# Regions on 512-byte starts, a constant made on GpSimd, first weights from the fifth unit on, and passes over 3, 5 and 8 slices, in an attention and two-layer MLP kernel

## The chip, the cores and the metric

One core of one Trainium2 chip runs the kernel. The metric is device time in microseconds (us), the median of the runs. [...]

## What is computed

```python
# 4 batches, 8 heads, 576 positions, head size 64
scores = (q @ k.T) / sqrt(64)
out = (scores * D) @ v            # D[i,j] = gamma_h**(i-j) for i >= j, else 0
x = out as [2304 tokens, 512]
h = x @ moe_w_in                  # 512 -> 2048
y = (h * sigmoid(1.702 * h)) @ moe_w_out     # 2048 -> 512
h2 = y @ moe2_w_in                # 512 -> 1024
s = h2 * softmax(h2)
z = (s - mean(s)) / sqrt(var(s) + 1e-6) * g_ln
return z @ moe2_w_out             # 1024 -> 512
```

All arrays are float32. The weights come to the device as float64 in 32-bit halves.

## The kernel before

**Attention.** There are 16 units, one for two heads of one batch. A unit is cut into four chunks of 128 positions and a rest of 64. `st0` scales v on ACT (L286, L287). `st2` makes the scores of the chunks on PE (L334) and masks them on DVE (L338). `states` makes the chunk states on PE (L298), which ACT scales out of PSUM (L304), and `st1` runs the scan over chunks on DVE (L314). `st4` puts the output together on PE (L355 with the masked scores, L367 to L378 with the scanned states), and DVE writes it into `xb` (L385, L390). In the loop over u in `run`, PE runs st2(u), L355 of unit u-1, states(u), and then L367 of unit u-1, which needs the scan of u-1, hence L304 of u-1. ACT, which takes its instructions in order, has st0(u+1) between the two: L304(u-1) stands behind it. Five input buffers (`NU`) hold units; unit u+4 is loaded when unit u-1 is done.

**First MLP layer.** The 2048 hidden columns are 16 weight slices. A slice's raw halves arrive in `wraw`. Three DVE instructions make float32 of 512 raw columns (`convert`: L208, L211, L214; six pieces for a slice), ACT rounds the 128x1024 result to float32r (L231, the "high" part w) and GpSimd subtracts for the "low" part (L236, twice 512 columns). This ACT and GpSimd work is called the split of a slice here. The pieces stand in a list `bg`; `background(n)` takes n DVE pieces from its front, and with them any splits that follow. Weights 0 to 7 are converted from the start; weights 8 to 15 replace them later. The tokens are six blocks of 384. A pass (`GENS`) takes all six blocks over a range of slices; a step is one slice of one block: 12 matmuls for h (L425), ACT sigmoid (L429), DVE product, high and low part (L430, L434, L435, into `gs`), then, one step later, 12 matmuls for y (L452). At a block's end y leaves PSUM (ACT L458 in the first pass, DVE L460 after it). The next block's x is split on ACT and GpSimd (L406, L407) in the last two steps of a block.

**Second layer.** h2 (L528) uses seven products in place of eight, with `ys` tiles as stationary operand (162 + 108 + 54 + 54 matmuls of 512 columns). After the normalization come transposes (L589), and the output o (L616) with the transposed tile `zs` as stationary operand: 17 token tiles with 24 matmuls of 512 columns, and the last with 48 of 256.

**Order and placement.** The order is written out by hand; the SP queue issues every load in program order. `mem` is one tile that is cut into regions by the table `_M` (constants, y, g, the attention buffers "att", three slots "t").

Of the kernel before, what the change touches and what calls it, by code (L numbers as in the profile page):

```python
# [9 lines left out]
F32 = mybir.dt.float32  # L10
# [7 lines left out]
B, H, S, D = 4, 8, 576, 64  # L18
NP = H // 2
# [4 lines left out]
P = 128  # L24
# [6 lines left out]
FH = NF // 2  # L31
GENS = ((0, 4), (4, 8), (8, 16))
NTT = NT // P
# [12 lines left out]
for _name, _w in (  # L46
    ("half", 1), ("g_ln", FB), ("vdec", NP * 3), ("step", NP), ("tri2", LAST), ("tri", CH), ("qdec", NP * CH),
    ("scan", NP * D * NCH),
):
    _CC[_name] = (_n, _n + _w)  # L50
    _n += _w

CCONST, _n_consts = _CC["scan"][0], _n


def constants():
# [22 lines left out]

    put("scan", step[:, :, None, None] * np.ones((D, 1)) * (np.arange(NCH) > 0))  # L80
    put("vdec", vdec / math.sqrt(D))
# [10 lines left out]

SLICE = 2 * DM
_M = {}
_n = 0
for _name, _w in (
    ("c", CCONST), ("y", NB * KB * TB), ("g", 2 * TB),
    ("att", 2 * CATT + 2 * NCH * D + 4 * NCH * CH + 2 * LAST), ("t", 3 * SLICE),
):
    _M[_name] = _n  # L100
    _n += _w
# [38 lines left out]
class Build:  # L140
    def __init__(self, tc, ctx, att, consts, ident_in, w1, w2in, w2out, out):
# [5 lines left out]
        self.wp = pool("wp")  # L147
        self.ctx, self.early, self.early_s = ctx, ExitStack(), ExitStack()
        self.gs = self.early_s.enter_context(
            tc.tile_pool(name="gsp", bufs=1, side="right", reuse_waits="tile")  # L150
# [26 lines left out]
    def load_decays(self, p, n):  # L177

        for name, at, w in (("scan", SCAN_AT, D * NCH), ("qdec", _M["c"] + _CC["qdec"][0], CH)):
            lo = _CC[name][0] + p * w  # L180
            self.load(at + p * w, self.const_in[:, lo:lo + n * w])

# [126 lines left out]
    def st1(self, u):  # L309

        st = self.un(u)[1]
        g = self.at(SCAN_AT + u % NP * D * NCH, D * NCH)
        st = self.at(ST_AT + (u % 2) * NCH * D, NCH * D)
        self.nc.vector.tensor_tensor_scan(st, g, st, 0.0, ALU.mult, ALU.add)  # L314
# [100 lines left out]
    def emit_h(self, gen, j, f, lo_engine, hi_act=False):  # L415
# [5 lines left out]
        for k in range(KB):  # L421
            x = self.xst[gen, j, k]
            w = slice(k * P, (k + 1) * P)
            for a, b in ((hi, 0), (lo, 0), (hi, 1)):
                nc.tensor.matmul(h[:, 0:TB], a[:, w], x[:, b], start=(n == 0), stop=(n == 3 * KB - 1))  # L425
                n += 1
        g = self.at(_M["g"] + (f % 2) * TB, TB)
        gs = self.gs[:, f % 2 * 2:f % 2 * 2 + 2]
        nc.scalar.activation(g, h[:, 0:TB], AF.Sigmoid, scale=1.702)  # L429
# [7 lines left out]
    def emit_y(self, gen, j, f):  # L437
        nc = self.nc
        hi, lo = self.w[f]
        gs = self.gs[:, f % 2 * 2:f % 2 * 2 + 2]  # L440
        first, last = f == GENS[gen][0], f == GENS[gen][1] - 1
# [183 lines left out]
    def run(self):  # L625
# [20 lines left out]
        for part in range(3):  # L646
            self.load_unit(0, part)
            if part == 0:
                self.load_consts()
        self.load_decays(0, 1)  # L650
        self.load_unit(1, 3)
        self.load_unit(1, 2)
        self.load_decays(1, NP - 1)
        for u in range(2, NU):
            self.load_unit(u, 3)
            self.load_unit(u, 2)
            if u != 3:
                load_w()

# [16 lines left out]
        for u in range(1, last + 2):  # L676
            if u <= last:
                self.st2(u)
                if u > 1:
                    self.background(1)  # L680
            else:

                while 0 not in self.split:
                    self.background(1)
                self.emit_h(0, 0, 0, nc.vector, True)
# [9 lines left out]
            if u < last - 1:  # L695
                self.st0(u + 2)
            if u % 2 == 0 or u > NU + 2:
                self.background(1)
# [5 lines left out]

        steps = [(g, j, f) for g, lo_hi in enumerate(GENS) for j in range(NB) for f in range(*lo_hi)]
        prev, held = None, []
        for g, j, f in steps:
            fl, n = f - GENS[g][0], GENS[g][1] - GENS[g][0]
# [6 lines left out]
            if g == 1 and j == 0 and fl == 1:  # L715

                for i in range(4):
                    first, *rest = self.split_weight(FH + i, T_LATER[i])
# [198 lines left out]
```

## Time and profile before

| | |
|---|---|
| median of 3 runs | 698.78 us (698.7 to 698.8) |
| the profiled execution's own time | 697.44 us |
| its span, first to last instruction | 695.7 us |
| busy: PE, DVE, ACT, POOL | 676.7, 512.0, 235.9, 225.8 us |
| DMA moved | 49.92 MB |

The profiled execution is 1.34 us under the median. PE is matmuls, PEld its weight loads, which run beside them; L numbers are lines of the kernel before. Up to about 75 us the core works on attention, to 482 us on the first layer, from there on the second.

### The profile page before, as it was taken

What the parts mean: (1) busy time and instruction counts of PE and PEld (TensorE: products, weight loads), DVE (VectorE), ACT (ScalarE), POOL (GpSimd) and SP (SyncE); (2) the same over time, 40 slices, a digit from 0 to 9 for tenths busy, and PEclk for the clock granted to TensorE, in tenths of its full rate; (3) what the DMA queues carried; (4) which work ended last, traced back from release to release, by engine and by line L of the source; (5) the groups of instructions that cost most, each with busy time, mean ns of one, the idle gap of its engine ahead of it and who ended that gap; (6) DMA issues with size and microseconds to landing.
All of it is one profiled execution on the core that took longest, in us unless ns stands there. A gap on an engine that the chain in (4) does not pass through costs nothing.

```text
span 695.7 us, 11260 instructions
## 1 busy us (share of the span) xinstructions
PE 676.7 (97%) x4454; PEld 629.6 (91%) x4454; DVE 512.0 (74%) x868; ACT 235.9 (34%) x496; POOL 225.8 (32%) x235
## 2 busy tenths in 40 slices
PE   7899999999999999999999999999998999999998
PEld 7888899999999999999999999998776788888887
DVE  2899847768788876636777777788698877877780
ACT  3554243333322233221212121254444424452331
POOL 0222154442232386520202030488633314331300
PEclk9999999999999999999999999999999999999999
DMA  9999500003232210001232210000000000000001
GB/s 325 419 341 373 201 1 1 1 1 103 81 91 91 78 44 1 1 1 60 62 96 64 84 61 1 1 1 4 2 15 16 16 30 32 30 16 16 30 32 46
DMA packets 13733, 49.92 MB, mean 72 GB/s; under 512 B 1520, under 2 KB 2544, under 8 KB 12272
## 3 DMA queue, kind: packets, MB, share of 16 engines
q1 hardware_dynamic: 13680, 49.20, 19.9%
q8 instruction: 35, 0.57, 0.3%
q14 instruction: 18, 0.15, 0.1%
HBM read 44.48 MB, written 4.72 MB: 71 GB/s over the span
## 4 chain that ended last, share of the span: by engine, by line
PE 80%; DVE 11%; ACT 3%; DMA 2%; issue 2%; POOL 1%; SPq 0%; POOLq 0%; DVEq 0%; ACTq 0%
PE yp L452 28%; PE h L425 27%; PE o L616 13%; PE h L528 9%; DMA mem<-in_att 2%; PE zT L589 2%; DVE mem L338 2%; DVE mem L568 1%; POOL xs L407 1%; DVE mem L314 1%; DVE mem L573 1%; DVE mem L208 1%; DVE mem L214 1%; DVE wraw L211 1%; ACT mem L566 1%
## 5 line engine op out<-in xcount | busy, mean ns | idle before, releaser
L452 PE MATMUL yp<-gs,w 128*128 128x384 f32 x1152 | 216.9, 337 | 0.7 <-DVE gs L435 0.6
L425 PE MATMUL h<-xs,w 128*128 128x384 f32 x1152 | 216.9, 337 | 0.6 <-POOL xs L407 0.3
L452 PEld LDWEIGHTS yp<-gs,w 128*128 128x128 f32 x1152 | 200.4, 188 | 3.4 <-DVE mem L460 1.8
L425 PEld LDWEIGHTS h<-xs,w 128*128 128x128 f32 x1152 | 201.0, 188 | 2.2 <-POOL xs L407 2.1
L407 POOL TENSOR_TENSOR xs<-xb,xs 128x384 fp32r<-128x384 f32 (+1 forms) x96 | 87.3, 934 | 253.2 <-ACT xs L406 253.2
L429 ACT ACTIVATE mem<-h 128x384 f32<-128x384 f32 x96 | 47.3, 493 | 267.8 <-PE h L425 267.6
L430 DVE TENSOR_TENSOR mem<-h,mem 128x384 f32<-128x384 f32 x96 | 53.4, 556 | 87.5 <-ACT mem L429 87.2
L616 PE MATMUL o<-w,zs 128*128 128x512 f32 (+1 forms) x456 | 105.1, 386 | 0.6 <-ACT zs L598 0.4
L616 PEld LDWEIGHTS o<-w,zs 128*128 128x128 f32 x456 | 81.1, 188 | 18.4 <-ACT zs L598 0.8
L435 DVE TENSOR_TENSOR gs<-mem,gs 128x384 fp32r<-128x384 f32 x96 | 80.3, 837 | 11.1 <-ACT gs L432 2.3
L236 POOL TENSOR_TENSOR w<-mem,w 128x512 fp32r<-128x512 f32 x40 | 55.9, 1422 | 64.9 <-ACT w L231 54.2
L434 DVE CAST gs<-mem 128x384 fp32r<-128x384 f32 x92 | 53.1, 577 | 9.1 <-PE yp L452 0.5
L489 POOL TENSOR_TENSOR ys_s<-mem,ys_s 128x256 fp32r<-128x256 f32 x36 | 33.9, 952 | 58.2 <-ACT ys_s L488 58.2
L528 PE MATMUL h<-wt,ys_s 128*128 128x512 f32 x162 | 41.6, 392 | 0.7 <-DVE mem L534 0.7
L534 DVE TENSOR_TENSOR mem<-h,mem 128x512 f32<-128x512 f32 x36 | 24.6, 688 | 22.6 <-PE h L528 13.4
L528 PEld LDWEIGHTS h<-wt,ys_s 128*128 128x128 f32 x162 | 30.2, 188 | 7.6 <-DVE mem L534 1.1
L406 ACT CAST xs<-xb 128x384 fp32r<-128x384 f32 (+1 forms) x96 | 35.5, 431 | 0.0
L576 POOL TENSOR_TENSOR mem<-mem 128x1 f32<-128x1 f32 x18 | 10.1, 559 | 69.3 <-DVE mem L575 61.5
L599 DVE TENSOR_TENSOR zs<-zT,zs 128x512 fp32r<-128x512 f32 x36 | 23.1, 683 | 8.8 <-ACT zs L598 8.8
L568 DVE TENSOR_TENSOR mem<-mem 128x1024 f32<-128x1024 f32 x18 | 25.3, 1406 | 4.9 <-ACT mem L566 4.9
L528 PE MATMUL h<-wb,ys_a 128*128 128x512 f32 x108 | 27.5, 390 | 0.0
L231 ACT CAST w<-mem 128x1024 fp32r<-128x1024 f32 x20 | 20.8, 1049 | 19.1 <-DVE mem L214 13.7
(78 smaller groups left out, 723.4 us busy)
## 6 DMA issues: line engine op xcount, KB each, us to landing
mem<-in_att SPq DMA_DIRECT2D x11, 1120.0 KB, 8.4
wraw<-in_w SPq DMA_DIRECT2D x16, 512.0 KB, 9.5
mem<-in_w SPq DMA_DIRECT2D x16, 512.0 KB, 3.7
out<-mem SPq DMA_DIRECT2D x17, 256.0 KB, 2.0
mem<-in_w2in SPq DMA_DIRECT2D x8, 512.0 KB, 3.8
mem<-in_w2out SPq DMA_DIRECT2D x8, 512.0 KB, 3.7
mem<-in_att SPq DMA_DIRECT2D x5, 544.0 KB, 8.0
mem<-in_att SPq DMA_DIRECT2D x4, 576.0 KB, 9.3
```

What stands on the lines that cost most here:

```text
L236: nc.gpsimd.tensor_tensor(lo[:, c], w[:, c], f32(hi[:, c]), ALU.subtract)
L406: nc.scalar.copy(t[:, 0, done:done + n], x)
L407: nc.gpsimd.tensor_tensor(t[:, 1, done:done + n], x, f32(t[:, 0, done:done + n]), ALU.subtract)
L425: nc.tensor.matmul(h[:, 0:TB], a[:, w], x[:, b], start=(n == 0), stop=(n == 3 * KB - 1))
L429: nc.scalar.activation(g, h[:, 0:TB], AF.Sigmoid, scale=1.702)
L430: nc.vector.tensor_tensor(g, h[:, 0:TB], g, ALU.mult)
L434: nc.vector.tensor_copy(gs[:, 0], g)
L435: lo_engine.tensor_tensor(gs[:, 1], g, f32(gs[:, 0]), ALU.subtract)
L452: nc.tensor.matmul(o, a[:, w], gs[:, b], start=(first and i == 0), stop=(last and i == 2))
L489: nc.gpsimd.tensor_tensor(ys[:, 1], src, f32(ys[:, 0]), ALU.subtract)
L528: nc.tensor.matmul(o, a[:, l, k], m[:, w], start=(start and i == 0), stop=(stop and i == 5), skip_group_check=True,)
L616: nc.tensor.matmul(o[:, 0:n], z[:, a, k], b[:, c:c + n], start=(k == 0 and i == 0), stop=(k == FB - 1 and i == 2),)
```

## The change

1. **Regions.** `mem` begins at byte 16512 of a partition. Each region of `_M` now begins at a multiple of 512 bytes (before: 128 bytes past one for the constants, 484 bytes past one for y, g, att and t). A pad of 480 bytes at the right end moves the tiles allocated there: `gs`, the x splits `xs`, `zs` and the last weight w19 (before: 480 bytes past a multiple of 512; now 0). The tiles of `w`, `wraw`, `xb` and `ys` lay at multiples of 512 bytes before and do so now.
2. **scan constants.** The 512 KB factor table of the scan is no longer loaded (before: 128 KB ahead of unit 1 and 384 KB ahead of unit 2). GpSimd fills it with one memset of 128x1024 and four copies of 128x64x3.
3. **First weights.** The first two loads of weight halves come after units 2 to 4, not between them. Background pieces begin at u = 4, one for an odd u and two for an even one (before: u = 2, two for u = 2, 4, 6 and each u from 8, else one).
4. **Passes** over slices 0 to 2, 3 to 7 and 8 to 15 (before 0 to 3, 4 to 7, 8 to 15), with g and gs buffers by the parity of the step, not of the slice.

```diff
-GENS = ((0, 4), (4, 8), (8, 16))
+GENS = ((0, 3), (3, 8), (8, 16))
+STEPS = [(g, j, f) for g, lo_hi in enumerate(GENS) for j in range(NB) for f in range(*lo_hi)]
+BUF = {s: i % 2 for i, s in enumerate(STEPS)}
...
-    ("scan", NP * D * NCH),
...
+LINE = 128
+MEM_SHIFT = 96
+RIGHT_PAD = 120
...
+    _n += (MEM_SHIFT - _n) % LINE
     _M[_name] = _n
...
+        pad = ctx.enter_context(tc.tile_pool(name="pad", bufs=1, side="right"))
+        self.pad = pad.tile([P, RIGHT_PAD], F32, name="pad")
...
-        for name, at, w in (("scan", SCAN_AT, D * NCH), ("qdec", _M["c"] + _CC["qdec"][0], CH)):
-            lo = _CC[name][0] + p * w
-            self.load(at + p * w, self.const_in[:, lo:lo + n * w])
+        lo = _CC["qdec"][0] + p * CH
+        self.load(_M["c"] + lo, self.const_in[:, lo:lo + n * CH])
+
+    def fill_scan(self):
+
+        nc = self.nc
+        nc.gpsimd.memset(self.at(SCAN_AT, NP * D * NCH), 0.0)
+        for p in range(NP):
+            g = self.at(SCAN_AT + p * D * NCH, D * NCH).rearrange("r (e c) -> r e c", c=NCH)
+            step = self.const("step")[:, p:p + 1].unsqueeze(2).to_broadcast([P, D, NCH - 1])
+            nc.gpsimd.tensor_copy(g[:, :, 1:], step)
...
-        g = self.at(_M["g"] + (f % 2) * TB, TB)
-        gs = self.gs[:, f % 2 * 2:f % 2 * 2 + 2]
+        b = BUF[gen, j, f]
+        g = self.at(_M["g"] + b * TB, TB)
+        gs = self.gs[:, b * 2:b * 2 + 2]
...
+        self.fill_scan()
         self.load_decays(0, 1)
...
             self.load_unit(u, 2)
-            if u != 3:
-                load_w()
+        load_w()
+        load_w()
...
-                if u > 1:
+                if u > 3:
                     self.background(1)
...
-            if u % 2 == 0 or u > NU + 2:
+            if u > 3 and u % 2 == 0:
                 self.background(1)
...
-                for i in range(4):
+                for i in range(GENS[0][1]):
                     first, *rest = self.split_weight(FH + i, T_LATER[i])
```

The SP queue at the start of the program, before (`in_att` are units: two rows for one unit; `in_consts` constants; `in_w` a half slice; the kernel's own lines):

```order
L171 DMA mem<-in_consts 128x256
L171 DMA mem<-in_consts 128x128
L171 DMA mem<-in_att 128x1152
L171 DMA mem<-in_att 128x1088
L171 DMA mem<-in_consts 128x768
L171 DMA mem<-in_consts 128x384
L171 DMA mem<-in_att 128x1152
L171 DMA mem<-in_att 128x1088
L195 DMA wraw_91<-in_w 128x1024
L171 DMA mem<-in_att 128x1152
```

and of the change, from the same place (the pair of 1152 and 1088 columns is units 1, 2, 3, 4 in turn):

```order
L179 DMA mem<-in_consts 128x128
L179 DMA mem<-in_att 128x1152
L179 DMA mem<-in_att 128x1088
L179 DMA mem<-in_consts 128x384
L179 DMA mem<-in_att 128x1152
L179 DMA mem<-in_att 128x1088
L179 DMA mem<-in_att 128x1152
L179 DMA mem<-in_att 128x1088
L179 DMA mem<-in_att 128x1152
L179 DMA mem<-in_att 128x1088
L211 DMA wraw_95<-in_w 128x1024 x2
```

The rows of 256 and 768 constant columns are gone, and the half slice that stood ahead of unit 3 stands behind unit 4.

DVE in the first pass, the end of one block of tokens and the begin of the next, before (h1_2 and h1_3 are the block's last two steps, h2_0 the next block's first, wraw5 and wraw6 slices in conversion):

```order
L430 TENSOR_TENSOR mem_60<-h1_2_1227,mem_60 128x384
L434 CAST gs_67<-mem_60 128x384
L435 TENSOR_TENSOR gs_67<-mem_60,gs_67 128x384
L211 SCALAR_TENSOR_TENSOR wraw5_96<-wraw5_96,mem_60 128x512
L214 SCALAR_TENSOR_TENSOR mem_60<-wraw5_96 128x512
L430 TENSOR_TENSOR mem_60<-h1_3_1258,mem_60 128x384
L434 CAST gs_67<-mem_60 128x384
L435 TENSOR_TENSOR gs_67<-mem_60,gs_67 128x384
L430 TENSOR_TENSOR mem_60<-h2_0_1293,mem_60 128x384
L434 CAST gs_67<-mem_60 128x384
L435 TENSOR_TENSOR gs_67<-mem_60,gs_67 128x384
L208 TENSOR_SCALAR mem_60<-wraw6_97 128x512
```

and of the change (h1_2 is the last of three steps):

```order
L446 TENSOR_TENSOR mem_60<-h1_2_1195,mem_60 128x384
L450 CAST gs_71<-mem_60 128x384
L451 TENSOR_TENSOR gs_71<-mem_60,gs_71 128x384
L227 SCALAR_TENSOR_TENSOR wraw4_99<-wraw4_99,mem_60 128x512
L230 SCALAR_TENSOR_TENSOR mem_60<-wraw4_99 128x512
L446 TENSOR_TENSOR mem_60<-h2_0_1232,mem_60 128x384
L450 CAST gs_71<-mem_60 128x384
L451 TENSOR_TENSOR gs_71<-mem_60,gs_71 128x384
L224 TENSOR_SCALAR mem_60<-wraw5_100 128x512
L227 SCALAR_TENSOR_TENSOR wraw5_100<-wraw5_100,mem_60 128x512
```

A block still carries the six pieces of one slice, but over three steps: the fourth step, which had no piece behind it, is gone.

## Rows read from the trace of the kernel before

**Rows 1.** Page, part 1: busy us, share of the span, instructions.
```profile
PE 676.7 (97%) x4454; PEld 629.6 (91%) x4454; DVE 512.0 (74%) x868; ACT 235.9 (34%) x496; POOL 225.8 (32%) x235
```
**Rows 2.** The chain that ended last: start us, us, what ran.
```profile
100.43 2.08 PE yp L452 x12
102.51 2.08 PE h L425 x12
...
571.97 5.59 PE o L616 x24
577.56 0.87 PE zT L589 x8
578.43 5.58 PE o L616 x24
584.02 9.57 PE h L528 x42
```
**Rows 3.** Windows: PE, PEld, DVE, ACT, POOL busy, PEclk, DMA share, GB/s.
```profile
5.00:35.00 30.00, 25.58 (x448) 23.10 (x446) 19.32 (x40) 15.45 (x33) 4.73 (x5) 1.00 1.02 404
93.00:110.00 17.00, 16.68 (x96) 16.12 (x95) 11.09 (x18) 7.25 (x18) 7.59 (x9) 1.00 0.00 0
545.00:690.00 145.00, 145.00 (x702) 120.03 (x701) 105.40 (x186) 56.76 (x118) 36.31 (x47) 1.00 0.07 26
```
**Rows 4.** Timeline of PE, attention: start us, us, instruction [idle before it <-releaser].
```profile
9.28 1.16 PE L334 MATMUL s<-mem 64*128 64x128 f32 x16 [0.55 <-DMA mem<-in_att]
13.32 0.99 PE L367 MATMUL o<-mem 64*64 64x128 f32 x12 [0.89 <-DVE mem L314]
14.66 1.16 PE L334 MATMUL s<-mem 64*128 64x128 f32 x16
23.04 0.99 PE L367 MATMUL o<-mem 64*64 64x128 f32 x12 [1.41 <-DVE mem L314]
28.62 1.16 PE L334 MATMUL s<-mem 64*128 64x128 f32 x16
36.14 0.98 PE L367 MATMUL o<-mem 64*64 64x128 f32 x12 [0.94 <-DVE mem L314]
37.47 1.16 PE L334 MATMUL s<-mem 64*128 64x128 f32 x16
41.39 1.16 PE L334 MATMUL s<-mem 64*128 64x128 f32 x16
71.44 1.16 PE L334 MATMUL s<-mem 64*128 64x128 f32 x16
79.05 0.99 PE L367 MATMUL o<-mem 64*64 64x128 f32 x12 [0.28 <-DVE mem L314]
```
**Rows 5.** Timeline of ACT, attention, the same columns.
```profile
19.66 1.06 ACT L286 ACTIVATE mem<-mem 128x256 f32<-128x256 f32 x2 [2.80 <-DMA mem<-in_att]
21.27 0.71 ACT L304 ACTIVATE mem<-T,mem 128x256 f32<-128x256 f32 x1
22.45 1.06 ACT L286 ACTIVATE mem<-mem 128x256 f32<-128x256 f32 x2 [0.47 <-DMA mem<-in_att]
...
33.15 1.05 ACT L231 CAST w<-mem 128x1024 fp32r<-128x1024 f32 x1 [1.66 <-DVE mem L214]
34.10 0.74 ACT L304 ACTIVATE mem<-T,mem 128x256 f32<-128x256 f32 x1
```
**Rows 6.** Waits: who for whom, us in total, times, longest.
```profile
ACT mem L286 <- DMA mem<-in_att: 18.2, 11, 4.7
ACT w L231 <- DVE mem L214: 13.7, 4, 5.7
```
**Rows 7.** DMA issues: how often, KB each, median us to landing.
```profile
wraw<-in_w SPq DMA_DIRECT2D x16, 512.0 KB, 9.5
mem<-in_consts SPq DMA_DIRECT2D x1, 384.0 KB, 7.1
mem<-in_consts SPq DMA_DIRECT2D x1, 128.0 KB, 4.6
```
**Rows 8.** Sources L236 and L435: count, ns min/median/max, first and last start.
```profile
L236 POOL TENSOR_TENSOR w<-mem,w x40: 1269/1307/2270, 34.3 to 497.7; 128x512 fp32r<-128x512 f32 x40
L435 DVE TENSOR_TENSOR gs<-mem,gs x96: 557/561/1568, 81.4 to 479.2; 128x384 fp32r<-128x384 f32 x96
```
**Rows 9.** Timeline of DVE and POOL in one block of the first pass.
```profile
97.55 0.36 DVE L434 CAST gs<-mem 128x384 fp32r<-128x384 f32 x1
...
100.10 2.56 POOL L236 TENSOR_TENSOR w<-mem,w 128x512 fp32r<-128x512 f32 x2 [4.33 <-ACT w L231]
...
101.66 1.22 DVE L434 CAST gs<-mem 128x384 fp32r<-128x384 f32 x1
```

More of the change, by code (lines that the diff above doesn't have):

```diff
@@ L51 @@
     _n += _w
-CCONST, _n_consts = _CC["scan"][0], _n
+CCONST = _n_consts = _n
 def constants():
@@ L78, in constants @@
     put("step", step)
-    put("scan", step[:, :, None, None] * np.ones((D, 1)) * (np.arange(NCH) > 0))
     put("vdec", vdec / math.sqrt(D))
@@ L309, in st1 @@
     def st1(self, u):
-        st = self.un(u)[1]
         g = self.at(SCAN_AT + u % NP * D * NCH, D * NCH)
@@ L439, in emit_y @@
         hi, lo = self.w[f]
-        gs = self.gs[:, f % 2 * 2:f % 2 * 2 + 2]
+        b = BUF[gen, j, f]
+        gs = self.gs[:, b * 2:b * 2 + 2]
         first, last = f == GENS[gen][0], f == GENS[gen][1] - 1
@@ L702, in run @@
             load_w()
-        steps = [(g, j, f) for g, lo_hi in enumerate(GENS) for j in range(NB) for f in range(*lo_hi)]
         prev, held = None, []
-        for g, j, f in steps:
+        for g, j, f in STEPS:
             fl, n = f - GENS[g][0], GENS[g][1] - GENS[g][0]
```

## Prediction

> **What bounds the kernel now.** Read the page's busy times first: PE works 676.7 us [rows 1] of a span of 695.7, so at most some 19 us stand in its gaps, and a change gains only by closing gaps or by making matmuls themselves shorter. The chain of waits then shows where PE runs without a gap: in the first layer twelve matmuls follow each other every 2.08 us, 173.3 ns each, y and h in turn [rows 2], and the window from 545 us on is all PE [rows 3]. Two places are left. One is the attention, where from 5 to 35 us PE is busy 25.58 of 30 us while the DMA engines have no pause (share 1.02, 404 GB/s) [rows 3]. The other, 482 to 545 us, is untouched by the change.
>
> In the attention, look at the starts of L334, one for each unit [rows 4]. The best pitch is 3.92 us (37.47 to 41.39, units 7 and 8). From unit 1 (9.28) to unit 5 (28.62) four pitches took 19.34, so 3.66 too much: 1.46 in the first, 2.20 in the next three. From unit 5 to unit 15 (71.44) ten took 42.82, 3.62 too much. PE waits in L367 for the scan (23.04, 36.14, 79.05 [rows 4]); the scan waits for ACT's L304, and L304 stands behind another ACT instruction. Early that is st0 of the next unit, which waits for its load: ACT was idle 2.80 us until 19.66, and L304 came at 21.27 [rows 5]. Later it is a split: L231 waited 1.66 us for DVE's last piece of the slice, ran 1.05 us, and L304 followed at 34.10 [rows 5]. Both kinds have their line in the waits: 18.2 us for loads, 13.7 us for four splits [rows 6].
>
> **The change, part by part.** The sum is made against the profiled execution, 697.44 us, 1.34 under the median of 698.78.
>
> *Loads.* Gone are 128 KB ahead of unit 1 and 384 KB ahead of unit 2; a half slice of 512 KB moves from ahead of unit 3 to behind unit 4 (sizes: [rows 7]). At 404 GB/s [rows 3] that is 0.32 us earlier for unit 1, 1.3 for unit 2, 2.6 for units 3 and 4, and 1.3 for unit 5, which queues behind the moved half as before. The queue passed is SP's alone; its loads of the halves wait for nothing there. PE's wait at 9.28 was for a load, so unit 1 starts 0.3 earlier. The excess of 1.46 stays: there ACT waits for unit 1's v, which comes only as much earlier as PE itself. The waits of st0 that ended at 19.66 and 22.45 [rows 5] end at about 17.1 and 19.9. L304 then follows 1.6 us later, at 18.7 and 21.5, and its scan some 1.5 us after that, while PE asks for them at about 20.9 and 24.8: L367 stands 1.33 us ahead of the next unit's start (36.14 to 37.47 [rows 4]), so 2.59 after its own at the best pitch, and units 3 and 4 now start at 18.3 and 22.2. So the 2.20 go but for about 0.2 at unit 5. Term: -0.3 - 2.2 + 0.2 = **-2.3 us**. Ends: -4.0 if the first pitch also becomes 3.92; 0 if the waits only change hands.
>
> *Constants on GpSimd.* The nearest row is GpSimd's 512 columns in 1.27 to 2.27 us [rows 8], a subtraction with two inputs. By it the memset of 1024 columns takes 2.5 to 4.5 us and four copies of 192 columns 1.9 to 3.4 together. GpSimd had no work then, the step column comes with the second load of the queue, and the first scan's user waited until 13.32 [rows 4]. Term: **0**, covered by that idle time; if the cover is gone, the first units slip by what it is late, at most a few tenths. No gain of its own remains beside the bytes counted above.
>
> *Pieces and splits.* Up to the end of attention DVE now does 18 pieces, not 25, and ACT three splits, not four: slices 0 to 2 are all that the first block needs. Splits now fall behind the last pieces of slices 0, 1 and 2, in the turns of units 7, 11 and 15. The four splits account for the 3.62 us above and the 0.28 at 79.05 [rows 4], about 1.0 each. One fewer gives 1.0, thinner pieces in the late turns perhaps 0.2 more: **-1.2 us**. Ends: 0, if three splits in a thinner list stall as long as four; -3.9, if none stalls.
>
> *Passes.* The steps and matmuls are the same in number; block ends too. What moves is the conversion of slices 3 to 7 into the first pass. A block there has three steps, 3 x 4.16 = 12.48 us, not 16.64, and still carries six pieces, one split and one x split. In the window of one such block DVE was busy 11.09 us for 18 instructions [rows 3], four steps of three and six pieces; 15 of 18 make 9.2 of 12.48 us. It fits, but the slack shrinks, and where GpSimd runs L236 the cast behind it takes 1.22 us and not 0.36 [rows 9]. y of a step begins a whole step after its h has ended, with another y and h between (the chain's turns [rows 2]), so most of this is hidden. I allow 0.1 us in each of five blocks: **+0.5 us**. Ends: 0 and the rival below. The parity buffers alternate as before, cost 0, hidden by the same alternation; if they didn't, h would wait for y in the odd passes.
>
> *Regions.* Do matmuls care where their operands begin? Twelve matmuls of L425 and L452, moving operand 480 bytes past a multiple of 512, stationary on one: 173.3 ns for 384 columns [rows 2], 13.3 over 384/2.4. L528, both operands on multiples: 9.57/42 = 227.9 ns for 512 columns, 14.5 over. So a misplaced moving operand costs nothing that shows, and two aligned ones don't collide. L616 has the stationary `zs` misplaced: 5.59/24 = 232.9 ns, 19.6 over [rows 2], in a stretch where PE never pauses [rows 3]. This is the one difference of placement between L528 and L616, so I take it for the cause: 408 matmuls x 5.0 ns = **-2.0 us**. Ends: 0 and -2.0; the 48 short ones are left at 0. The other engines' operands in `mem` were misplaced in all their rows, so no row prices them; off PE's chain I take 0.
>
> [...]
>
> **Sum:** 697.44 - 2.3 - 1.2 + 0.5 - 2.0 = 692.4; plus 1.34 the median comes to **693.8 us**. Attention then ends about 3.5 us earlier and the whole remaining program moves up with it.
>
> **Rivals.**
> - *The placement is without effect.* L616 stays at 232.9 ns, because its longer interval comes from its own accumulation and not from zs. For it: L616 and L528 differ in the PSUM use too. Against: L425 also puts 12 in one bank and has no such surplus. 695.8 us.
> - *The queue stays the bound.* The DMA share of 1.02 [rows 3] says that loads are late by bytes, not by order: only the 512 KB saved count, 1.3 us, and three splits stall as long as four, with the placement without effect. 698.78 - 1.3 = 697.5. Against: the half slice really stood ahead of units 3 and 4.
> - *Attention runs nearly clean*: splits hardly stall once pieces are thin, -3.9 in place of -1.2, no loss in the passes: 690.6.
> - *DVE becomes the bound in the first pass* (slower). Its 15 instructions average 9.2/15 = 0.62 us; at 0.83 they fill the block. If every second one is held up like the cast (1.22 [rows 9]; L435 shows up to 1.57 [rows 8]), a block takes 8 x 1.22 + 7 x 0.62 = 14.1, 1.6 over, 8.1 in five blocks: 695.8 - 0.5 + 8.1 = 703.4. From 0.7 us for each block on it eats the 3.5 of attention. For it: GpSimd's split and x split of a block now come within three steps. Against: in the old block of [rows 9] only the stretch beside L236 is slow.
>
> [...]
>
> **How the numbers follow.** Forecast 0.42; placement without effect 0.27; queue the bound 0.13; clean attention 0.08; DVE bound 0.10. A measurement can tell 0.2% (1.4 us) from no change. Faster is the forecast, the second and the clean case, and a little of the queue case: 0.78; within 0.2% most of the queue case: 0.12; slower 0.10. The range reaches from the clean case to the queue case, 690.5 to 697.6, and leaves out the DVE case and the outermost of the bounds; the likeliest case alone is 692.5 to 695.
>
> **What would show it.** L334 starts at about 18.3 and 22.2 for units 3 and 4 and 26.2 for unit 5; ACT's waits for in_att fall from 18.2 to under 13 us; three L231 before 76 us; h of the first step at about 72 us; L616's 24 matmuls in about 5.47 us in the chain, L425 and L452 still 2.08. Wrong if the first h still comes after 74.5 us, if y in the first pass waits for gs by more than 1 us in sum, or if L616 stays at 5.59 (then the second case).

## The result, and the profile after

The changed kernel takes **689.82 us** (median of 4 runs, 689.74 to 690.27) against 698.74 (698.64 to 698.80) for the kernel before, run beside it: ratio 0.9879, 95% interval 0.9867 to 0.9891. That is 8.9 us faster; 693.8 was forecast, and the measured time lies 0.7 us below the range's lower end.

The profiled execution took 689.74 us, span 688.0, with a granted TensorE clock of 1.000 (before: 0.999). In the changed file the lines stand 15 to 17 further down: L334 is now L349, L367 L382, L304 L320, L286 L302, L314 (the scan) L329, L231 L247, L236 L252, L425 L440, L452 L469, L528 L545, L616 L633, and the pieces L208, L211, L214 are L224, L227, L230. A run that adds lines shifts them once more.

Start with the page's busy times, against [rows 1]:

```profile
PE 673.9 (98%) x4454; PEld 630.1 (92%) x4454; DVE 507.6 (74%) x869; ACT 233.0 (34%) x495; POOL 228.1 (33%) x240
```

PE is busy 2.8 us less with as many matmuls, so some matmuls became shorter; the rest of the 7.7 us of span was gaps. Three points of PE's trace divide the program: the first h of layer 1, the last y, the last o.

```
                first h    first h to last y    last y to last o    profiled time
before           75.36          406.72               210.27             697.44
changed          69.88          406.35               208.31             689.74
difference       -5.48           -0.37                -1.96              -7.70
```

Behind the last o the changed kernel takes 0.1 us more.

The attention is where most went. The same two windows as in [rows 3], then the units' starts on PE's timeline, against [rows 4]:

```profile
5.00:35.00 30.00, 28.13 (x484) 25.60 (x484) 20.66 (x44) 15.37 (x36) 4.03 (x4) 1.00 1.02 409
93.00:110.00 17.00, 17.00 (x100) 17.00 (x99) 14.23 (x21) 7.00 (x15) 11.06 (x10) 1.00 0.00 1
```
```profile
9.38 1.16 PE L349 MATMUL s<-mem 64*128 64x128 f32 x16 [0.33 <-DMA mem<-in_att]
...
13.37 0.99 PE L382 MATMUL o<-mem 64*64 64x128 f32 x12 [0.96 <-DVE mem L329]
...
14.71 1.16 PE L349 MATMUL s<-mem 64*128 64x128 f32 x16
...
18.62 1.16 PE L349 MATMUL s<-mem 64*128 64x128 f32 x16
...
22.54 1.16 PE L349 MATMUL s<-mem 64*128 64x128 f32 x16
...
38.19 1.16 PE L349 MATMUL s<-mem 64*128 64x128 f32 x16
...
42.31 1.16 PE L349 MATMUL s<-mem 64*128 64x128 f32 x16
```

From 14.71 on every pitch is 3.91 or 3.92 us, except two of 4.12 (above) and 4.09 (54.05 to 58.14), each with a split. The first pitch, 5.33, kept its excess. Unit 5 started at 26.45 and unit 15 at 65.97: units 1 to 5 took 17.07 us (19.34 before), units 5 to 15 39.52 (42.82 before). So of the 7.3 us that the attention lost before 5.5 are gone, not 3.5.

In the last layer the chain of waits, against [rows 2]:

```profile
572.04 5.46 PE o L633 x24
577.49 9.53 PE h L545 x42
587.89 5.49 PE o L633 x24
```

24 matmuls of L633 fell from 5.59 to 5.46 and 5.49 us, as forecast; h of this layer stayed (9.57, now 9.53).

### The profile page after: what moved, and what is told of

Read it like the earlier page. It is cut to its first block, busy times and chain, and to the rows that moved or that the text cites. A ratio compares the mean times of both kernels' runs of the same rounds, so it can differ in the third digit from the quotient of the medians.

```text
span 688.0 us, 11277 instructions
## 1 busy us (share of the span) xinstructions
PE 673.9 (98%) x4454; PEld 630.1 (92%) x4454; DVE 507.6 (74%) x869; ACT 233.0 (34%) x495; POOL 228.1 (33%) x240
## 4 chain that ended last, share of the span: by engine, by line
PE 82%; DVE 8%; DMA 3%; ACT 2%; issue 2%; POOL 2%; SPq 1%; DVEq 0%; POOLq 0%; ACTq 0%
PE yp L469 28%; PE h L440 28%; PE o L633 12%; PE h L545 9%; DMA mem<-in_att 3%; PE zT L606 2%; POOL xs L422 1%; DVE mem L585 1%; PE o L382 1%; PE o L370 1%; DVE mem L590 1%; PE s L349 1%; DVE mem L329 1%; DVE mem L353 1%; ACT mem L583 1%
## 5 line engine op out<-in xcount | busy, mean ns | idle before, releaser
L440 PE MATMUL h<-xs,w 128*128 128x384 f32 x1152 | 216.9, 335 | 1.0 <-POOL xs L422 0.8
L469 PE MATMUL yp<-gs,w 128*128 128x384 f32 x1152 | 216.3, 335 | 0.6 <-DVE gs L451 0.6
L440 PEld LDWEIGHTS h<-xs,w 128*128 128x128 f32 x1152 | 201.0, 188 | 3.0 <-POOL xs L422 2.9
L469 PEld LDWEIGHTS yp<-gs,w 128*128 128x128 f32 x1152 | 200.7, 188 | 2.4 <-DVE mem L477 1.4
L422 POOL TENSOR_TENSOR xs<-xb,xs 128x384 fp32r<-128x384 f32 (+1 forms) x96 | 88.7, 948 | 232.6 <-ACT xs L421 232.6
L633 PE MATMUL o<-w,zs 128*128 128x512 f32 (+1 forms) x456 | 103.2, 382 | 0.6 <-ACT zs L615 0.4
L633 PEld LDWEIGHTS o<-w,zs 128*128 128x128 f32 x456 | 81.2, 188 | 16.5 <-ACT zs L615 0.8
L451 DVE TENSOR_TENSOR gs<-mem,gs 128x384 fp32r<-128x384 f32 x96 | 78.8, 820 | 11.0 <-ACT gs L448 1.7
L252 POOL TENSOR_TENSOR w<-mem,w 128x512 fp32r<-128x512 f32 x40 | 55.0, 1400 | 75.0 <-ACT w L247 75.0
L545 PE MATMUL h<-wt,ys_s 128*128 128x512 f32 x162 | 41.5, 391 | 0.7 <-DVE mem L551 0.7
L545 PEld LDWEIGHTS h<-wt,ys_s 128*128 128x128 f32 x162 | 30.2, 188 | 7.5 <-DVE mem L551 1.2
L616 DVE TENSOR_TENSOR zs<-zT,zs 128x512 fp32r<-128x512 f32 x36 | 23.1, 684 | 8.4 <-ACT zs L615 8.4
L545 PE MATMUL h<-wb,ys_a 128*128 128x512 f32 x108 | 27.4, 389 | 0.0
L247 ACT CAST w<-mem 128x1024 fp32r<-128x1024 f32 x20 | 20.9, 1051 | 16.2 <-DVE mem L230 9.3
```

Of the source, the lines that this page charges most:

```text
L252: nc.gpsimd.tensor_tensor(lo[:, c], w[:, c], f32(hi[:, c]), ALU.subtract)
L422: nc.gpsimd.tensor_tensor(t[:, 1, done:done + n], x, f32(t[:, 0, done:done + n]), ALU.subtract)
L451: lo_engine.tensor_tensor(gs[:, 1], g, f32(gs[:, 0]), ALU.subtract)
L469: nc.tensor.matmul(o, a[:, w], gs[:, b], start=(first and i == 0), stop=(last and i == 2))
L545: nc.tensor.matmul(o, a[:, l, k], m[:, w], start=(start and i == 0), stop=(stop and i == 5), skip_group_check=True,)
L633: nc.tensor.matmul(o[:, 0:n], z[:, a, k], b[:, c:c + n], start=(k == 0 and i == 0), stop=(k == FB - 1 and i == 2),)
```

## The experiments

Eighteen variants ran, in four groups; each time is a median, beside the kernel before on the same chip (697.95 to 698.29 us). "First h" is the start of the first h in the profiled execution: the length of the attention. It varies: the changed kernel has 69.88, c1 and e3, whose attention is the same instructions in the same order, 70.38 and 70.71. So a few tenths of it count only where a single pitch or the medians bear them out.

### Where operands begin

`mem` is what the other engines work on; `zs`, `xs` and `gs` stand on the right side and move with the pad; `w`, `xb` and `ys` follow `mem`.

**a1_regions_back**: both parts of the alignment out of the changed kernel.

```
-    _n += (MEM_SHIFT - _n) % LINE
-        pad = ctx.enter_context(tc.tile_pool(name="pad", bufs=1, side="right"))
-        self.pad = pad.tile([P, RIGHT_PAD], F32, name="pad")
```

> The changed kernel with the old placement alone (regions and right-hand tiles back at 484 and 480 bytes past a multiple of 512). Theory, placement acts on PE's stationary operand only: L633's 24 matmuls go from 5.46-5.49 back to 5.58-5.59 us in the chain, the profiled time rises by 2.0 us to about 691.7, attention and first layer unchanged (first h at 69.9 us). Rival, placement also sped DVE, ACT or GpSimd in attention: first h comes later than 70.5 us and the profiled time rises by more than 3 us.

**a2_right_back**: the two lines of the pad alone out.

> Only the right-hand tiles (gs, xs, zs, w19) back at 480 past 512, the regions of mem stay on multiples of 512. Theory: the same 2.0 us as with both back, since zs alone costs; the profiled time about 691.7. Rival, the regions of mem carry the gain: 689.7 to 690.2.

**a3_weights_off32**: a tile of 32 bytes ahead of the weights.

```
+        self.shift = pool("shift").tile([P, 8], F32, name="shift")
         self.wp = pool("wp")
```

> A tile of 32 bytes ahead of the weight pool moves w, wraw, xb and ys 32 bytes past a multiple of 512; nothing else. Theory, a stationary operand that begins 32 bytes past a multiple of 64 costs 5 to 6 ns for each matmul whatever its width: L440 and L469 go from 173.3 to about 179 ns, 2304 x 5.5 = 12.7 us, and L545 from 226.9 to 232, 378 x 5.5 = 2.1 us: the profiled time about 704. Rival 1, only matmuls of 512 columns pay: plus 2.1 us, 691.8. Rival 2, it was something of zs other than its place: no change, 689.7.

**a4_right_64**: `RIGHT_PAD = 104`.

> The right-hand tiles 64 bytes past a multiple of 512. Theory, the step that counts is 64 bytes or less: L633 stays at 5.46 to 5.49 us for 24, profiled time 689.7. Rival, it is the 512 bytes: 5.58 to 5.59, 691.7.

Measured: a1 693.06 us, a2 691.57, a3 691.42, a4 691.34. All four have the final matmuls at 233 to 234 ns (last layer 209.8 to 210.3 us), and h and y of both layers as they were. Without the alignment (a1) the median is 3.2 us higher, more than the 2.0 expected; the profiled execution shows 2.0 in the last layer, 0.4 in the attention and 0.3 in layer 1. The regions of `mem` are part of it: a1 against a2, which differ in them alone, is 693.06 (692.50 to 693.35) against 691.57 (691.45 to 691.60), 0.9 apart in the profiled executions. ACT's scaling of v shows them, in the changed kernel and in a1:

```profile
13.97 0.91 ACT L302 ACTIVATE mem<-mem 128x256 f32<-128x256 f32 x2 [1.45 <-DMA mem<-in_att]
```
```profile
14.30 1.06 ACT L299 ACTIVATE mem<-mem 128x256 f32<-128x256 f32 x2 [1.40 <-DMA mem<-in_att]
```

All 16 pairs take 0.86 to 0.91 us where `mem` is aligned (changed, a2, e4) and 1.01 to 1.07 where it isn't (before, a1, c2).

For the matmuls, a3 and a4 speak against the step on which the forecast rested. (a3's time is near its first rival, but the final matmuls slowed, not h.) The chain of a3, where `zs` stands on a multiple of 512 as in the changed kernel and only the weights have moved, and where h has *both* its operands at 32:

```profile
549.98 5.59 PE o L634 x24
555.57 9.55 PE h L546 x42
```

The stationary operand is in place and the matmul is slow (5.59); both are off and it is quick (h, 227 ns). So neither place by itself counts. The next theory: moving and stationary operand must begin at the *same* offset. Two runs test it where the theories differ most.

**c1_both_32**: a3 and `RIGHT_PAD = 112`, every operand at 32.

> The changed kernel with every operand of TensorE moved by the same 32 bytes: w, xb, ys at 32 mod 512 (by a tile of 32 bytes ahead of them, as in the run with the weights alone at 32) and zs, xs, gs at 32 too (right pad 448 bytes). No work differs. Theory, formed on the runs so far: a 512-column matmul takes 227 ns where its moving and its stationary operand begin at the same offset of 512 bytes, 233 to 234 where they don't. Then L633 has 227 ns, layer 2 takes 208.2 to 208.6 us, 689.6 to 690.0 in all. Rival (each operand has to begin on a multiple of 512): L633 at 234 and the second layer's h at 234 as well, 691.4 or more.

**c2_before_w480**: the kernel *before* with a tile of 120 words ahead of the weights, so that these share the 480 of `zs`.

```
+        self.shift = pool("shift").tile([P, 120], F32, name="shift")
         self.wp = pool("wp")
```

> The kernel before with one tile of 480 bytes ahead of the weights and nothing else: w, xb and ys now begin at 480 mod 512, where zs, xs and gs stand already; mem, the loads, the turns and the passes are as before. Theory (equal offsets count, not multiples of 512): the final matmuls go from 232.9 to 227 ns, the second layer's h stays at 227, layer 2 goes from 210.3 to 208.3 us, and the time falls by 1.8 to 2.2 us, ratio 0.997. Rival (multiples of 512 count): the final matmuls stay at 233 and the second layer's h, with both operands at 480, goes to 233 too, the time rises by about 2 us.

c1: 690.22 us, final matmuls 227 ns. The last layer is 208.26, as in the changed kernel; the 0.4 that it is behind stand in the attention (first h 70.38), within what that varies by. c2: 696.09 against 697.95, ratio 0.9971 (0.9961 to 0.9981), last layer 208.43:

```profile
577.63 5.47 PE o L617 x24
583.10 9.52 PE h L529 x42
```

One tile that misplaces the weights by 480 bytes gives the kernel before the whole gain of the final matmuls. The equal start decides.

**e3_zs_sweep**: a single execution; the place of `zs` differs from token tile to token tile, `w` at 0.

```
-        z = self.zsp.tile([P, 2, FB, P], F32R, tag="zs", name=f"zs{t}", bufs=2)
+        z = self.zsp.tile([P, 2 * FB * P + 128], F32R, tag="zs", name=f"zs{t}", bufs=2)
+        o = ZS_OFF[t]
+        z = z[:, o:o + 2 * FB * P].rearrange("r (a b e) -> r a b e", a=2, b=FB)
```

> The changed kernel, w at 0 mod 512, with the tile of normalised rows placed differently in each of the 18 token tiles of the last matmul: 0, 16, 32, 64, 96, 128, 160, 192, 256, 320, 384, 416, 448, 480, 496, 0, 256 and 512 bytes past a multiple of 512. Read is the interval of 512-column matmuls for each tile. Theory: 227 ns at 0 and 512, 233 to 234 at 32, 64 and 480 (all seen); at 128, 256 and 384 either 233 as well (equal offsets modulo 512 are needed) or 227 (a coarser line counts); at 16 and 496 as at 32. Rival (it is not the relative offset but something else that the shift of whole regions brought): all tiles alike.

The chain, for the tiles at 16, 256, 320, 448, 496 and 0 bytes:

```profile
519.00 5.62 PE o L636 x24
...
595.57 5.46 PE o L636 x24
...
611.42 5.60 PE o L636 x24
...
640.42 5.51 PE o L636 x24
...
662.82 5.47 PE o L636 x24
669.17 5.46 PE o L636 x24
```

The mean interval of the 512-column matmuls, tile by tile, from the trace:

```
bytes   0     16    32    64    96    128   160   192   256   320   384   416   448   480   496
ns    227.9 233.5 233.3 233.3 234.3 232.4 233.2 229.0 227.1 233.4 233.1 234.1 229.2 233.4 227.6
```

(In the changed kernel the tiles have 226.7 to 228.5.) The pattern repeats after 256 bytes (64 and 320, 192 and 448 alike). Equal modulo 256 is quick; 16 bytes below (496) is quick too, 16 above is not; 64 below (192, 448) lies between, while 32 below (480) is slow. From the quickest row to the slowest it is 7.2 ns a matmul (227.1 to 234.3). What inside the chip does this, no run shows.

**e4_regions_alone**: the kernel before with the alignment of the change and nothing else of it.

> The kernel before with the aligned regions alone (the three constants, the line in the table of regions and the pad on the right). Loads, turns and passes as before. Theory: layer 2 falls by 2.0 us to 208.3, attention by 0.0 to 0.4, layer 1 by 0.0 to 0.3: 695.5 to 696.3, ratio 0.997. Rival (the gain of layer 2 hangs on the other parts): layer 2 stays at 210.3 and the time within 0.5 us of before.

695.12 against 698.29, ratio 0.9955 (0.9940 to 0.9970): 3.2 us, as much as a1 showed from the other side and more than I expected. Last layer 208.27 (-2.0), first h 74.86 (-0.5), layer 1 406.42 (-0.3). The interval reaches down to 2.1 us, first h varies by as much, and c2, with `mem` as before, has the same layer 1 (406.40): how much beyond the last layer the alignment is worth, e4 doesn't show; a1 against a2 does.

### The queue

**b3_halves_between**: the halves queued between the units again.

```
-        load_w()
-        load_w()
+            if u != 3:
+                load_w()
```

> The changed kernel with the weight halves queued again between the units (one half slice of 512 KB ahead of unit 3, ahead of unit 4 and so on), as before. Theory: unit 3 and unit 4 wait for 512 KB each at 404 GB/s, 1.3 us; units 3 and 4 start 1.3 us later and unit 5 about 1.3 to 2.6 later than 26.45; first h at 71.2 to 72.2, 691.1 to 692.2. Rival (the loads are hidden since the scan constants no longer come over the queue): within 0.4 us of 69.88 and 689.8.

**b4_constants_loaded**: no `fill_scan`; the scan's constants in the table and over the queue as before.

> The changed kernel with the scan's constants loaded over the queue as before (128 KB ahead of unit 1, 384 KB ahead of unit 2) and not made by GpSimd. Theory (bytes ahead of the units count one to one): unit 2 and later 1.3 us later, first h at 71.0 to 71.4, 690.9 to 691.3. Rival 1 (unit 2's load has slack, 14.71 is set by the first units' chain): within 0.3 us of 689.8. Rival 2 (GpSimd's fill delays the first scan, which waited for it by the trace in 0.96 us of PE idle): first pitch becomes 0.3 to 0.9 shorter, time between 689.0 and 689.8.

b3: first h 70.73, 690.53 us; b4: 71.31, 690.86. So +0.85 and +1.43 of attention; the sum, 2.28, is what the term *Loads* said (2.3). Only 0.7 and 1.0 us of it showed in the medians. b3's 0.85 is one pitch, 4.77 (18.64 to 23.41); of b4's 1.43 some 0.5 stand in two later pitches (4.13 and 4.43) that c1 and e3 have too, so that part isn't the loads.

**c3_constants_first** aims at the first pitch, the only large stall left:

```
-        self.st0(1)
         self.st2(0)
         self.states(0)
+        self.st0(1)
```

> The changed kernel with the first stage of unit 1 put behind the states of unit 0 in the program (two lines of the first section exchanged), so that ACT doesn't wait for unit 1's load ahead of unit 0's scan. Theory (the first pitch's 1.4 us of excess is ACT in order: unit 0's states stand behind unit 1's load): first pitch 4.4 to 4.9 in place of 5.33, first h at 69.0 to 69.5, 688.9 to 689.4. Rival (unit 1's own v then comes later by as much): first pitch 5.2 to 5.6, 689.7 to 690.1.

689.80 us, no gain. The first pitch did fall, to 4.21 (9.18 to 13.39), by more than I expected; the next were 4.26 and 4.55 and gave it back. The timeline of ACT shows what is behind it: unit 2's and 3's v were not there.

```profile
13.70 0.91 ACT L302 ACTIVATE mem<-mem 128x256 f32<-128x256 f32 x2 [2.06 <-DMA mem<-in_att]
...
17.62 0.91 ACT L302 ACTIVATE mem<-mem 128x256 f32<-128x256 f32 x2 [2.15 <-DMA mem<-in_att]
```

ACT's order sets the first pitch, the loads set the four units together.

### Splits and turns

The background has two turns in a unit: the first behind the unit's scores (`st2`), ahead of its states and scan, the second behind its scan. A slice has six pieces on DVE, and its split on ACT (L247) follows the sixth. The change moves the turns as well: the first from unit 4 on (before: from 2), the second at even units from 4 on (before: all even units, and every unit from 8 on). The forecast counted the pieces that this gives, 18 for 25, and didn't ask in which turn a split falls.

**b2_old_cadence**: the changed kernel with the old rule.

```
-                if u > 3:
+                if u > 1:
-            if u > 3 and u % 2 == 0:
+            if u % 2 == 0 or u > NU + 2:
```

> The changed kernel with the background's old turns (a piece after every unit from 2 on, a second one at even units, and two each at the end). Three splits stay, the lists are the same, only the turns come earlier and closer together. Theory (early and dense turns make ACT's split wait for DVE's piece and the scan's state behind it): splits stall about 0.9 us each again, first h at 72 to 73 us, 692 to 693 in all. Rival (the loads alone cleaned the attention; the splits stalled because units were late): first h stays within 0.4 us of 69.88 and the time within 0.5 of 689.8.

697.39 us: nearly all of the gain is gone, more than the theory allowed. Part of it is not the rule: the halves now come behind all units, and the early turns wait for them.

```profile
21.38 0.43 DVE L224 TENSOR_SCALAR mem<-wraw 128x512 uint32<-128x512 uint32 x1 [3.80 <-DMA wraw<-in_w]
```

**d1_old_turns_old_halves**: b2 with the queue of b3, which takes that wait away.

> The changed kernel with the background's old turns and with the halves queued between the units as before, so that the pieces of the early turns find their data (with the old turns alone DVE waited 3.8 us for a half near 21 us). What is left of the change in the attention: three splits for four and the scan's constants on GpSimd. Compare with the halves alone put back: first h 70.73, 690.53. Theory (turns that come early and close together make ACT's split wait for DVE's last piece): three splits stall 0.7 to 1.4 us each, first h at 73.0 to 75.0, 693 to 695. Rival (the old turns hurt only because the halves came late): first h at 70.5 to 71.7, 690.3 to 691.5.

694.98 us, first h 74.55; against b3 (690.53, 70.73) that is 4.5 us, 3.8 of it in the attention and 0.9 in layer 1 (PE waits 0.32 us for a scan at 78.26 and 1.00 at 86.99 for a product that stood behind four pieces on DVE; b3 waits once, 0.31). Three slices are needed, as in the changed kernel, and yet the attention is nearly as slow as before: the *turns* cost what I had put down to the fourth split. (They also do more: d1 converts a fourth slice, as before did, whose split falls behind the first h, at 75.24.) Which of them?

**e1_late_pairs**: the changed kernel with `if u > 3 and (u % 2 == 0 or u > NU + 2)`.

> The changed kernel with the old rule for the last turns alone (two pieces after every unit from unit 8 on, in place of two after every second one); no early turns, halves and constants as changed. Theory (DVE's time per unit: two pieces make 4.6 us of DVE work against a pitch of 3.91): units from about 50 us on with two pieces take 4.6 us each, with a split 5.0; first h 2.0 to 3.5 us later than 69.88, at 71.9 to 73.4. Rival (the early turns did the harm, the late ones are covered): first h at 69.9 to 70.6.

**e2_early_turns**: b3 with `u > 1` and `u % 2 == 0`, without the late pairs.

> The changed kernel with the halves queued between the units as before and the early turns alone put back (a piece after unit 2 and on, two at even units); from unit 4 on the turns are those of the changed kernel. Compare with the halves alone put back: first h 70.73, 690.53. Theory (DVE, as it stands, has no slack to catch up in): a delay of the early units stays to the end, first split near 32 us with a stall of about 1.4 us, first h at 71.8 to 73.0, 691.5 to 692.8. Rival (early pieces are hidden in DVE's idle time while the units wait for loads): first h at 70.3 to 71.2.

e2: 692.02 us, first h 72.03, as expected: 1.3 us for the early turns. e1: 689.95 us, first h 69.87; **the theory of DVE's budget falls.** With two pieces in every unit from 8 on the pitch stays at 3.91. DVE is busy all of it, and that is enough:

```profile
58.13:62.04 3.91, 3.91 (x76) 3.65 (x72) 3.91 (x10) 1.72 (x4) 0.00 (x0) 1.00 0.99 388
```

and the same work, ten instructions, took 4.61 us in d1:

```profile
52.48:57.09 4.61, 4.10 (x76) 3.78 (x72) 4.61 (x10) 1.63 (x5) 0.00 (x0) 1.00 0.94 367
```

(Columns as in [rows 3].) What differs is where the last piece of a slice falls. The kernel before, a late split, first ACT, then DVE and GpSimd:

```profile
48.98 1.04 ACT L231 CAST w<-mem 128x1024 fp32r<-128x1024 f32 x1 [3.10 <-DVE mem L214]
49.93 0.72 ACT L304 ACTIVATE mem<-T,mem 128x256 f32<-128x256 f32 x1
```
```profile
48.26 0.69 DVE L214 SCALAR_TENSOR_TENSOR mem<-wraw 128x512 uint32<-128x512 uint32 x1
...
50.68 1.23 DVE L314 TENSOR_TENSOR_SCAN mem<-mem 128x256 f32<-128x256 f32 x1 [0.80 <-ACT mem L304]
51.84 1.43 DVE L208 TENSOR_SCALAR mem<-wraw 128x512 uint32<-128x512 uint32 x1
```

The sixth piece (48.26) took the unit's *first* turn, ahead of the scan. ACT's split waits for it, the unit's states (L304) stand behind the split, and DVE idles 0.80 us for its scan. Behind the split GpSimd subtracts (L236, 2.88 us from 50.10 on), and beside it the scan takes 1.23 us and the next piece 1.43, where 0.68 and 0.41 are usual. Counted by the old rule, pieces 6, 12, 18 and 24 all take a first turn (units 5, 9, 12 and 15). Were the sixth piece in the *second* turn, the scan would be past. e1 fits: by its rule piece 6 takes a first turn, and the pitch there is 4.43 (38.05 to 42.48); pieces 12 and 18 take second turns, and every later pitch is 3.91.

But the place isn't all. In the changed kernel pieces 6, 12 and 18 take first turns too (units 7, 11 and 15), and the scan is as late,

```profile
53.09 0.68 DVE L230 SCALAR_TENSOR_TENSOR mem<-wraw 128x512 uint32<-128x512 uint32 x1
...
55.52 1.24 DVE L329 TENSOR_TENSOR_SCAN mem<-mem 128x256 f32<-128x256 f32 x1 [0.81 <-ACT mem L320]
56.67 1.26 DVE L353 TENSOR_TENSOR mem<-s,mem 128x512 f32<-128x512 f32 x2
```

and yet the pitch is only 4.09. Two things set what a late split costs, in the rows of all runs from unit 7 on. One is when the last piece starts, against the next unit's start on PE: 0.97 to 0.94 us ahead of it the next pitch is 4.07 to 4.12; 0.63 ahead, 4.43 (e1, c1, e3); 0.28 ahead, 4.76 (f1); 0.02 ahead, 5.01 (before, 61.80 against 61.82). The other is a second piece in the same unit, behind the late scan: with it the pitch after that is 4.60 or 4.61, without it 3.91. In the changed kernel no second piece stands there (the masks, L353, follow at once), and the last pieces start 0.95 ahead. So thinner turns make a late split cheap, and a second turn makes it free; the change did the first, e1 and f1 the second.

**f1_before_shifted_turns**: the kernel *before*, one turn left out at the start, so that slices 1 to 3 end in second turns.

```
-                if u > 1:
+                if u > 2:
```

> The kernel before with one comparison changed: the first turn of the background after unit 2 is left out (u > 2 in place of u > 1), so that every later piece comes one turn later; the number of turns in the late units, the loads and the passes stay. Theory, new after the late pairs alone cost nothing: what counts is in which of a unit's two turns the last piece of a slice falls. In the first turn (ahead of that unit's states and scan) ACT's split waits for it and the unit's states wait behind the split, the scan comes 0.8 to 0.9 us late, and the pieces beside GpSimd's subtraction slow down; in the second turn (behind the scan) all of this is hidden. With the shift, slices 1 to 3 end in second turns and slice 0 still in a first one: the first split still stalls by about 1 us, the pitches from 49 us on become 3.9 to 4.0 in place of 4.07, 4.60, 5.02 and 4.60; first h at 72.0 to 73.2 in place of 75.0 to 75.4, ratio 0.995 to 0.997. Rival (four splits at this rate stall wherever they fall, DVE being full): first h within 0.5 us of before, ratio 0.999 to 1.001.

696.84 against 698.14, ratio 0.9974 (0.9963 to 0.9984). Where it was to work, it did. A late split, ACT and then DVE:

```profile
53.14 1.05 ACT L231 CAST w<-mem 128x1024 fp32r<-128x1024 f32 x1 [1.55 <-DVE mem L214]
54.09 0.74 ACT L304 ACTIVATE mem<-T,mem 128x256 f32<-128x256 f32 x1
```
```profile
51.84 0.68 DVE L314 TENSOR_TENSOR_SCAN mem<-mem 128x256 f32<-128x256 f32 x1
52.44 0.67 DVE L214 SCALAR_TENSOR_TENSOR mem<-wraw 128x512 uint32<-128x512 uint32 x1
...
55.50 0.81 DVE L314 TENSOR_TENSOR_SCAN mem<-mem 128x256 f32<-128x256 f32 x1
```

The scan at 51.84 is past when the split begins, the next one waits for nothing, and PE's units 9 to 15 start every 3.92 us:

```profile
47.09 1.16 PE L334 MATMUL s<-mem 64*128 64x128 f32 x16
51.01 1.16 PE L334 MATMUL s<-mem 64*128 64x128 f32 x16
...
70.61 1.16 PE L334 MATMUL s<-mem 64*128 64x128 f32 x16
```

These six pitches took 23.52 us, 26.13 before (45.31 to 71.44): 2.6 us, two splits in each, so 1.3 on average for a split that moves by one turn. The first h, though, came at 74.83, not at 72.0 to 73.2: units 1 to 9 became 1.5 us slower. A wait for a load took 0.6 of it (a pitch of 5.99 for 5.40), and the first split, still in a first turn and now with a second piece behind it in its unit, 0.9 (pitches 4.76 and 4.60).

**f2_odd_second_turns**: the changed kernel with `u % 2 == 1`; all three slices end in second turns.

> The changed kernel with the second turn of the background after odd units in place of even ones; as many pieces up to each split but for one turn. By the same theory all three splits of the attention end in second turns, and the 0.2 to 0.5 us that the first and the second still cost (pitches 4.12 and 4.09) go: first h at 69.2 to 69.7 in place of 69.88, 689.0 to 689.6 in all. Rival (the stall that is left comes from something else, or the first block pays for it): 689.6 to 690.4.

690.45 us. The attention does what the theory says: every pitch after the first is 3.91 to 3.93, first h 69.15. The first block gives it back: x's own splits there are late, layer 1 takes 407.05 us. The second wait below is in the changed kernel too, and the y behind it starts at 85.70 there and at 85.71 here.

```profile
84.32 0.79 PE L440 MATMUL h<-xs,w 128*128 128x384 f32 x3 [0.47 <-POOL xs L422]
85.42 0.45 PE L440 MATMUL h<-xs,w 128*128 128x384 f32 x1 [0.32 <-POOL xs L422]
```

### The passes

**b1_four_slices**: `GENS = ((0, 4), (4, 8), (8, 16))`.

> The changed kernel with passes over 4, 4 and 8 slices again, so that the attention has four weight splits (and 24 thinner pieces) in place of three. Measured in the changed kernel: pitch 3.91 us, with 0.2 us extra at each of two splits, first h at 69.88 us, layer 1 406.35 us. Theory (what made the splits stall was the list of pieces, which now begins later and thins out): a fourth split costs as little as the other three only if its pieces still fit; I expect first h at 70.1 to 71.0 us, layer 1 within 0.4 of 406.35, 690.0 to 691.2 in all. Rival 1 (each split costs about 1 us, as the prediction's term says, and the third was hidden): first h at 71 to 72, 691 to 692. Rival 2 (the narrower first pass is what gains in layer 1): layer 1 over 406.7.

692.53 us. The attention is as short (first h 70.06), layer 1 is 2.6 us longer. At the new rate the fourth slice isn't ready when the first block asks for it, on PE's timeline:

```profile
83.83 0.44 PE L440 MATMUL h<-xs,w 128*128 128x384 f32 x1 [0.64 <-ACT w L247]
85.66 2.20 PE L440 MATMUL h<-xs,w 128*128 128x384 f32 x11 [1.39 <-POOL w L252]
...
91.69 0.79 PE L440 MATMUL h<-xs,w 128*128 128x384 f32 x3 [0.36 <-POOL xs L422]
92.98 0.44 PE L440 MATMUL h<-xs,w 128*128 128x384 f32 x1 [0.50 <-POOL xs L422]
```

So the pass over three slices is what lets the turns be few, and neither does it alone. No variant is faster than the changed kernel beyond what the runs tell apart (c3 689.80, e1 689.95).

## Why the prediction was wrong, step by step

- *Loads*, -2.3: right in size (units 1 to 5 took 2.27 us less; b3 and b4 give 2.28 by the first h, 1.7 by the medians). Units 3 to 5 started at 18.62, 22.54 and 26.45 where 18.3, 22.2 and 26.2 were named; the 0.3 is unit 1, which started at 9.38 and not earlier. One sign failed: ACT's waits for in_att were to fall from 18.2 to under 13 us and are 18.6. ACT still waits for its loads, but from unit 2 on these waits no longer reach PE.
- *Constants on GpSimd*, 0: right. The memset took 0.95 us and the four copies 1.22 together, done at 4.60, far ahead of the first scan, which waited for ACT until 12.63.
- *Pieces and splits*, -1.2: **this step failed**; units 5 to 15 show -3.3. "The four splits account for the 3.62 us above, about 1.0 each. One fewer gives 1.0" took a split for the cost. Only three of the four came ahead of the first h (33.15, 48.98 and 62.51; the fourth at 76.05), and the runs give a split no price of its own: f1 keeps all four and loses 2.6 us less by moving two of them one turn; e1 does more pieces than the changed kernel and its attention is as short (69.87); and the two that the changed kernel has left among its units cost 0.2 each, in the same first turns. What costs is a last piece that comes late in its unit, ahead of the scan, with a second piece behind it. The rows were there: L304 behind the split in [rows 5]. What I left out was to read the diff's two lines on the turns against that order. My "ends", 0 and -3.9, held the result, and the rival *attention runs nearly clean* had its reason, thinner pieces; I gave them 0.2 us. That it would come so near to -3.9 no row told.
- *Passes*, +0.5: layer 1 became 0.37 shorter. Between a1, which has the passes without the alignment, and before it is 0.1, so the passes cost nothing that shows. The rival with DVE as the bound didn't come: the block's window shows DVE 14.23 of 17.00 us and PE without a pause.
- *Regions*, -2.0: the size of the final matmuls is right (-1.96), **the cause is not.** "The stationary zs is misplaced, so I take it for the cause": a3 is slow with `zs` in place, c1 and c2 are quick with it misplaced. h and o differed in two things, the place of `zs` and that h's operands begin alike; I named the first and saw only that. The 2.4 by which the step divides the columns is a rate that the changed kernel's trace shows: its matmuls of 256, 384 and 512 columns follow each other every 120, 173 and 227 ns (medians), so 128 more columns take 53 and 54 ns, 2.4 columns in a ns. With the wrong cause went "off PE's chain I take 0": ACT's scaling of v became 0.15 us shorter in every unit, and a1 against a2 shows 1.5 us in the medians for `mem` alone.
- The 1.34 us from the profiled execution to the median: before's runs lie between 697.3 and 699.3 in the later comparisons, its profiled one near the lower end; the changed kernel's lie within 0.6 us and its profiled one is the lowest. So the offset belonged to before's scatter, not to the kernels, and 1.3 of the 4.0 us by which the forecast was off came from it. Of the other 2.7, 2.0 are the attention and 0.9 layer 1; the last layer was right.

Open: by which path the alignment of `mem` shortens the whole program, and what in the chip makes the equal start quick.

## What to carry to other kernels

When background work is threaded through a loop, look at what stands *behind* its last step on each engine it uses: the same split cost about 1.3 us ahead of the unit's scan and nothing behind it (f1), and ahead of the scan with thinner turns 0.2 to 0.5 (the changed kernel, c1, e3). Take a difference between two rows for a cause only after listing everything in which they differ; a rival that moves the other operand costs one tile. An offset between a profiled execution and a median is the scatter of that kernel until several runs of both say otherwise.

## What was not expected of the hardware

A 512-column matmul took 227 ns where its moving and its stationary operand began alike modulo 256 bytes, and 232 to 234 where they didn't, with the exceptions of the table (16 bytes below 227.6, 64 below 229.0 and 229.2). Matmuls of 384 columns kept 173 ns in every placement tried, and those of 256 columns went the other way by a little, 120 ns with equal starts and 117 to 118 without (a4, before). Units in which DVE was busy to the last tenth of a microsecond (e1, 3.91 of 3.91 us) took no longer for it. A pair of 128x256 scalings on ACT took 0.15 us longer (1.06 against 0.91) where its region of `mem` began 484 bytes past a multiple of 512 than where it began on one.
